# Attention scores as 64x64 products on quarters of the array, in place of 128x128 products on block-diagonal queries

## The chip, the cores and the metric

The kernel runs on one core of a Trainium2 chip. The metric is device time in microseconds, from the first to the last instruction of one execution as the chip reports it. Three runs of the kernel before took 924.23, 922.78 and 923.79 us, so the median is 923.79 us. Engine names are those of the profile: PE multiplies matrices (PEld is its weight load), DVE does elementwise work and reductions, ACT evaluates functions and copies, POOL is the general-purpose engine, and SP issues most transfers.

## The reference

Inputs are q, k and v of shape 8 x 8 x 576 x 64 (batch, heads, sequence, head dimension) in float32, and four weights in float64. The first step is windowed causal attention:

```
scores = scale * np.matmul(q, k.transpose(0, 1, 3, 2))
rel = pos[:, None] - pos[None, :]
mask = (rel >= 0) & (rel < 64)
scores = np.where(mask, scores, -1000000000.0)
scores = scores - np.max(scores, axis=-1, keepdims=True)
attn = np.exp(scores)
attn = attn / (np.sum(attn, axis=-1, keepdims=True) + 1e-09)
x = np.matmul(attn, v)
```

Its output, 8 batches of 576 tokens with 512 channels, goes through a token-mixing and then a channel-mixing network:

```
h = np.maximum(xt @ w_tok1, 0.0) @ w_tok2      # over the 576 tokens, hidden 256
u = x + h.transpose(0, 2, 1)
h2 = np.maximum(u @ w_ch1, 0.0) @ w_ch2        # over the 512 channels, hidden 1536
out = u + h2
```

## The kernel before

The work has two phases. The **first phase** does attention and token mixing, and converts the float64 weights to float32 pieces. The **second phase** is channel mixing, 9 chunks of 512 tokens, with products split into high and low parts (names ending in hi and lo).

In the first phase the sequence of each batch is cut into 9 blocks of 64 tokens. A **tile** holds two blocks on 128 partitions, rows 0-63 and rows 64-127 (`tile_blocks`), with all 8 heads; two batches make 9 tiles, and there are 36 tiles. Since the window is 64, a block of queries needs its own block of keys and the one before it, 128 keys.

- **Scores** (`qk`, L248-260). One product contracts over 128 partitions: partitions 0-63 hold the head dimension of the first block and partitions 64-127 that of the second. So that the two blocks do not mix, the queries are copied into `qbd`, a buffer that is block-diagonal: for each head 128 columns, the first 64 with the first block's queries on partitions 0-63, the last 64 with the second block's on partitions 64-127, and zeros elsewhere. The zeros are written once (L117, L118); the two copies per tile (`expand_q`, L155 and L156) are DVE's. A tile has 8 products, one for each head, in two halves u of 4 heads; each half fills one PSUM bank (tag "s", two buffers).
- **Softmax** (L262-287). For the first 7 tiles the mask is added on PE by a product (L255), later by DVE (L275); DVE takes the row maximum (L278, or L272 and L273), and ACT the exponentials (L286) with their sums.
- **Transposes** on PE (L293) with a copy by ACT (L295) give `pt`, and the product with v (`av`, L305) gives the tile's output `xp`. It is done as 16 products of 64 output rows, one for each head and block. DVE divides by the sums (L313, L314, L319).
- **Token mixing**: `split_x` splits the result (ACT L90, POOL L93), `tok1` (L349) and the *pieces* of `tok2` (L384, L391, copied out by ACT in L396) do the two products. A batch has 8 pieces, 4 of 256 tokens and 4 of 320; a tile does up to two, one behind its first transposes and one behind `av`.
- **Weights**: each tile converts one slice of the weights, on DVE in two parts (L187-189 and L198-201), then on POOL (L203) and on ACT and POOL (L90, L93).

Order is by hand: each engine executes what the loop over tiles (L448-531) records, in that order. An iteration i does the scores and softmax of tile i + 1 and the rest of tile i. On PE the order is: scores u = 0, transposes u = 0, a piece, scores u = 1, transposes u = 1, `tok1`, `av`, a piece. On ACT it is: copy of the first `pt`, casts, exponentials u = 0 of the next tile, copy of the piece, copy of the second `pt`, exponentials u = 1, copy of the second piece, cast of the tile's result. On DVE it is: mask and maximum u = 0, the two copies into `qbd`, reciprocal, first part of a weight slice, mask and maximum u = 1, second part of the slice, division. In the first four tiles both transposes come together and the copies into `qbd` come last.

Of the kernel before, what the change touches and what calls it, by code (L numbers as in the profile page):

```python
# [10 lines left out]
F32 = mybir.dt.float32  # L11
# [11 lines left out]
P = 128  # L23
BLK = 64
# [12 lines left out]
# Columns of a tile's keys that the first load brings, parts that the last product comes in.  # L37
K0 = P + BLK
# [20 lines left out]
# A batch's blocks in the order in which the kernel holds its tokens: tile t has blocks t and t + 4,  # L59
# the last block shares a tile with the other batch of its pair.  # L60
# [13 lines left out]
def mixer_kernel(ctx: ExitStack, tc: tile.TileContext, qh, kh, kr, vh, wt1, wt2, wc1, wc2, out):  # L74
# [34 lines left out]
    with ExitStack() as actx:  # L109
# [5 lines left out]
        qbd = [pq.tile([P, H, 2, BLK], F32, name=f"qbd{n}") for n in range(3)]  # L115
        def zero_q(qt, eng):
            eng.memset(qt[0:BLK, :, 1], 0.0)  # L117
            eng.memset(qt[BLK:P, :, 0], 0.0)  # L118

        zero_q(qbd[0], nc.vector)  # L120
        kbs, loaded, cpool = {}, {}, [pq]

        def load_k(i):
            p, t = divmod(i, TPP)
            if t == 4:
                kt = pq.tile([P, H, P], F32, name=f"kr{p}", tag="kr", bufs=1)
                nc.sync.dma_start(kt, kr[p])
                kbs[i] = kt
            elif t in (0, 5):
                b = 2 * p + (t == 5)  # L130
                kt = pq.tile([P, H, 5 * BLK], F32, name=f"k{b}", tag="k", bufs=2)
                if b != 0:
                    nc.sync.dma_start(kt, kh[b])
                for n in range(4):
                    kbs[i + n] = kt[:, :, n * BLK:n * BLK + P]
                return kt

        def load_q(i):
            qr = pq.tile([P, H, BLK], F32, name=f"q{i}", tag="q", bufs=3)
            if i == 0:  # L140
                for hs in (slice(0, 4), slice(4, H)):
                    nc.sync.dma_start(qr[:, hs], qh[i, :, hs])
                    nc.sync.dma_start(k0[:, hs, :K0], kh[0, :, hs, :K0])
            else:
                nc.sync.dma_start(qr, qh[i])
            loaded[i] = [qr, None]
# [5 lines left out]

        def expand_q(i, h0=0, h1=H):
            qr, qt = loaded[i][0], qbd[i % 3]
            nc.vector.tensor_copy(qt[0:BLK, h0:h1, 0], qr[0:BLK, h0:h1])  # L155
            nc.vector.tensor_copy(qt[BLK:P, h0:h1, 1], qr[BLK:P, h0:h1])  # L156
# [17 lines left out]
        zero_q(qbd[1], nc.gpsimd)  # L174
        zero_q(qbd[2], nc.gpsimd)
# [5 lines left out]
        def to_f32_a(raw, n, tag):  # L181
            """float64 words, low and high, to the nearest float32: its range, and the mantissa in place."""
# [10 lines left out]
        def to_f32_b(c, low, high, n, tag):  # L193
            """Its sign and exponent, and what the low word adds."""
# [11 lines left out]
        # Weights: (source, where its high and low parts or its float32 go, columns).  # L206
# [41 lines left out]
        def qk(i, u):  # L248
            qt, kt = qbd[i % 3], kbs[i]
            tag, bufs = ("up", 1) if i < N_PE and (2 * i + u) % 3 == 2 else ("s", 2)  # L250
            s = ps.tile([P, 4, P], F32, name=f"s{i}_{u}", tag=tag, bufs=bufs)
            on_pe = i < N_PE
            if on_pe:
                mk = maskr[1 if tile_blocks(i)[0][1] == 0 else 0]
                nc.tensor.matmul(s, identr, mk.unsqueeze(1).to_broadcast([P, 4, P]), start=True, stop=False,  # L255
                                 skip_group_check=True)
            for h in range(4):
                nc.tensor.matmul(s[:, h], qt[:, 4 * u + h].rearrange("p a q -> p (a q)"), kt[:, 4 * u + h],  # L258
                                 start=not on_pe, stop=True, skip_group_check=on_pe)
            s_ps[i, u] = s  # L260

        def softmax(i, u):  # L262
# [7 lines left out]
            nmu = nm[:, 4 * u:4 * u + 4]  # L270
# [9 lines left out]
        def softmax_exp(i, u):  # L280
# [3 lines left out]
            for h in range(4):  # L284
                g = 4 * u + h
# [14 lines left out]
        def av(i, pts):  # L300
            vt = loaded.pop(i)[1]
            xp = ps.tile([P, H, D], F32, name=f"xp{i}", tag="av", bufs=1)
            for h in range(H):
                for half in range(2):
                    nc.tensor.matmul(xp[half * BLK:(half + 1) * BLK, h],  # L305
                                     pts[h // 4][:, h % 4, half * BLK:(half + 1) * BLK],
# [141 lines left out]
        for i in range(-1, NT + 1):  # L448
# [14 lines left out]
            if i + 1 < NT:  # L463
                qk(i + 1, 0)
# [187 lines left out]
```

## Time and profile before

The profile is of one execution; its span is 923.1 us, and the median of the runs shown is 0.7 us above it.

| | us |
|---|---|
| median of 3 runs | 923.79 |
| lowest, highest | 922.78, 924.23 |
| span of the profiled execution | 923.1 |
| first `av` of the 36 | at 14.2 |
| last `av` of the 36 | at 295.8 |
| first product of the second phase | at 312.6 |
| PE, DVE, ACT, POOL busy in the span | 892.4, 425.6, 304.3, 134.0 |

A line of the timeline gives the start, the duration, the engine, the line of the program, the operation, what is written and read, the shapes, and how many instructions were merged (xN). A bracket at the end tells how long the engine sat idle before it and what released it. The line of a helper stands for all its uses, so L90 and L93 are the high and low parts of every split. The end of a PE instruction is modelled and overlaps the next; rates on PE are therefore taken from starts.

### The profile page before, as it was taken

What the parts mean: (1) busy time and instruction counts of PE and PEld (TensorE: products, weight loads), DVE (VectorE), ACT (ScalarE), POOL (GpSimd) and SP (SyncE); (2) the same over time, 40 slices, a digit from 0 to 9 for tenths busy, and PEclk for the clock granted to TensorE, in tenths of its full rate; (3) what the DMA queues carried; (4) which work ended last, traced back from release to release, by engine and by line L of the source; (5) the groups of instructions that cost most, each with busy time, mean ns of one, the idle gap of its engine ahead of it and who ended that gap; (6) DMA issues with size and microseconds to landing.
All of it is one profiled execution on the core that took longest, in us unless ns stands there. A gap on an engine that the chain in (4) does not pass through costs nothing.

```text
span 923.1 us, 13509 instructions
## 1 busy us (share of the span) xinstructions
PE 892.4 (97%) x5426; PEld 737.4 (80%) x5426; DVE 425.6 (46%) x762; ACT 304.3 (33%) x953; POOL 134.0 (15%) x134
## 2 busy tenths in 40 slices
PE   6899899899999988999999999999999999999998
PEld 5778788788888867888888888888888888888887
DVE  7999999999998494022131130130130120220210
ACT  5677677676776422021020020120120120120210
POOL 4334334433233162000000000000000000000000
PEclk9999999999999999999999999999999999999999
DMA  9556565765862640110200200100200100100000
GB/s 338 176 195 239 185 212 201 240 217 179 281 212 90 206 144 18 40 40 12 80 1 23 69 1 23 68 1 23 69 1 34 58 1 35 57 10 26 12 12 34
DMA packets 41661, 89.07 MB, mean 96 GB/s; under 512 B 5504, under 2 KB 19200, under 8 KB 39680
## 3 DMA queue, kind: packets, MB, share of 16 engines
q1 hardware_dynamic: 39488, 86.39, 27.8%
q10 hardware_dynamic: 2112, 1.84, 0.6%
q8 instruction: 42, 0.69, 0.3%
q14 instruction: 19, 0.16, 0.1%
HBM read 67.37 MB, written 20.84 MB: 96 GB/s over the span
## 4 chain that ended last, share of the span: by engine, by line
PE 71%; DVE 26%; issue 1%; ACT 1%; DMA 1%; POOL 0%; SPq 0%; DVEq 0%; ACTq 0%; POOLq 0%
PE op L609 32%; PE gp L575 30%; DVE nm L278 3%; DVE e L275 3%; PE up L391 3%; DVE qbd L156 3%; DVE qbd L155 2%; DVE c L198 2%; PE h L349 2%; DVE c L189 2%; DVE r L201 2%; DVE x L319 1%; DVE c L188 1%; PE s L258 1%; PE up L384 1%; DVE r L200 1%
## 5 line engine op out<-in xcount | busy, mean ns | idle before, releaser
L579 ACT ACTIVATE ghi<-gp 128x512 fp32r<-128x512 f32 x108 | 64.4, 598 | 464.1 <-PE gp L575 463.2
L575 PE MATMUL gp<-uhi,w1hi 128*128 128x512 f32 x432 | 171.0, 396 | 6.0 <-DVE glo L580 6.0
L575 PE MATMUL gp<-uhi,w1lo 128*128 128x512 f32 x432 | 173.6, 402 | 0.0
L575 PE MATMUL gp<-ulo,w1hi 128*128 128x512 f32 x432 | 171.4, 397 | 0.0
L609 PE MATMUL op<-glo,w2hi 128*128 128x512 f32 (+1 forms) x444 | 170.3, 384 | 0.0
L609 PE MATMUL op<-ghi,w2hi 128*128 128x512 f32 (+1 forms) x444 | 170.3, 384 | 0.0
L609 PE MATMUL op<-ghi,w2lo 128*128 128x512 f32 (+1 forms) x444 | 170.2, 383 | 0.0
L580 DVE SCALAR_TENSOR_TENSOR glo<-gp,ghi 128x512 fp32r<-128x512 f32 x108 | 74.4, 690 | 198.9 <-ACT ghi L579 198.8
L611 DVE TENSOR_TENSOR uf<-op,uf 128x512 f32<-128x512 f32 (+1 forms) x37 | 25.0, 677 | 263.6 <-PE op L609 263.6
L286 ACT ACTIVATE e<-e,nm 128x128 f32<-128x128 f32 x232 | 90.4, 391 | 54.9 <-DVE nm L278 54.9
L575 PEld LDWEIGHTS gp<-uhi,w1hi 128*128 128x128 f32 x432 | 81.8, 189 | 27.4 <-DVE glo L580 8.1
L575 PEld LDWEIGHTS gp<-ulo,w1hi 128*128 128x128 f32 x432 | 81.7, 189 | 20.9
L575 PEld LDWEIGHTS gp<-uhi,w1lo 128*128 128x128 f32 x432 | 81.7, 189 | 19.0
L609 PEld LDWEIGHTS op<-ghi,w2hi 128*128 128x128 f32 x444 | 83.4, 188 | 16.6
L609 PEld LDWEIGHTS op<-glo,w2hi 128*128 128x128 f32 x444 | 83.4, 188 | 16.5
L609 PEld LDWEIGHTS op<-ghi,w2lo 128*128 128x128 f32 x444 | 83.4, 188 | 16.5
L258 PE MATMUL s<-k,qbd 128*128 128x128 f32 x512 | 71.5, 284 | 4.4 <-DVE qbd L156 2.5
L258 PEld LDWEIGHTS s<-k,qbd 128*128 128x128 f32 x512 | 66.3, 199 | 7.4 <-DVE qbd L156 2.8
L203 POOL TENSOR_TENSOR w<-r,c 128x384 f32<-128x384 f32 (+1 forms) x39 | 38.7, 991 | 167.0 <-DVE r L201 142.8
L305 PEld LDWEIGHTS xp<-v,pt 128*64 128x64 f32 x1152 | 37.4, 140 | 13.3 <-issue 3.9
L93 POOL TENSOR_TENSOR xlo<-x,xhi 128x512 fp32r<-128x512 f32 x32 | 41.4, 1293 | 25.4 <-ACT xhi L90 25.1
L391 PE MATMUL up<-t2hi,hhi 128*128 128x320 f32 (+1 forms) x128 | 43.7, 342 | 0.0
(78 smaller groups left out, 1099.3 us busy)
## 6 DMA issues: line engine op xcount, KB each, us to landing
v<-vh SPq DMA_DIRECT2D x36, 512.0 KB, 3.7
raw<-wc SPq DMA_DIRECT2D x32, 384.0 KB, 4.2
q<-qh SPq DMA_DIRECT2D x35, 256.0 KB, 4.1
k<-kh SPq DMA_DIRECT2D x7, 1280.0 KB, 9.8
out<-uf SPq DMA_DIRECT2D x35, 256.0 KB, 2.4
uf<-u_dram SPq DMA_DIRECT2D x8, 1024.0 KB, 5.7
u_dram<-u SPq DMA_DIRECT2D x7, 512.0 KB, 3.5
kr<-kr SPq DMA_DIRECT2D x4, 512.0 KB, 5.4
```

Source lines behind the costliest of these rows:

```text
L93: eng_lo.tensor_sub(lo, src, hi.bitcast(F32))
L156: nc.vector.tensor_copy(qt[BLK:P, h0:h1, 1], qr[BLK:P, h0:h1])
L203: nc.gpsimd.tensor_add(w, rf, cf)
L258: nc.tensor.matmul(s[:, h], qt[:, 4 * u + h].rearrange("p a q -> p (a q)"), kt[:, 4 * u + h], start=not on_pe, stop=True, skip_group_check ...
L275: nc.vector.scalar_tensor_tensor(out=e, in0=s_ps.pop((i, u)), scalar=scale, in1=mk.unsqueeze(1).to_broadcast([P, 4, P]), op0=ALU.mult, op1 ...
L286: nc.scalar.activation(e[:, h], src[:, h], AF.Exp, bias=nm[:, g:g + 1], scale=by, accum_out=sm[:, g:g + 1])
L305: nc.tensor.matmul(xp[half * BLK:(half + 1) * BLK, h], pts[h // 4][:, h % 4, half * BLK:(half + 1) * BLK], vt[:, half, h], start=True, sto ...
L391: nc.tensor.matmul(up[:, :n], hx[:, cs], w[:, tt * S + s0:tt * S + s0 + n], start=False, stop=(k == 6), skip_group_check=True)
L575: nc.tensor.matmul(gp, w[:, ct * F + ft * P:ct * F + (ft + 1) * P], x[:, ct], start=(k == 0), stop=(k == 3 * NCT - 1))
L579: nc.scalar.activation(ghi, gp, AF.Relu)
L580: nc.vector.scalar_tensor_tensor(out=glo, in0=gp, scalar=0.0, in1=ghi.bitcast(F32), op0=ALU.max, op1=ALU.subtract)
L609: nc.tensor.matmul(op, w[:, ft, cs], x[:, cols], start=(k == 0), stop=(k == 3 * NFT - 1))
```

## The change

The host lays queries and keys out by the parity of the head: partitions 0-63 hold the even heads, partitions 64-127 the odd ones, each with all the blocks of a batch for the keys and both blocks of a tile for the queries. A score product now contracts over 64 partitions and has 64 query rows: it takes one quarter of the array, by the head's parity (which partitions are read) and by the block in the tile (which PSUM partitions are written). A tile has 16 such products of 64x64 with 128 keys moving, where it had 8 of 128x128. Both PSUM banks of a tile are filled in one go (even heads in one, odd heads in the other), ahead of the first transposes. `qbd`, its zeros, `expand_q` and the separate key tensor `kr` are gone; u now means parity, and `av` takes its heads alternately from the two `pt`.

```
-        def qk(i, u):
-            qt, kt = qbd[i % 3], kbs[i]
-            tag, bufs = ("up", 1) if i < N_PE and (2 * i + u) % 3 == 2 else ("s", 2)
-            s = ps.tile([P, 4, P], F32, name=f"s{i}_{u}", tag=tag, bufs=bufs)
...
-            for h in range(4):
-                nc.tensor.matmul(s[:, h], qt[:, 4 * u + h].rearrange("p a q -> p (a q)"), kt[:, 4 * u + h],
-                                 start=not on_pe, stop=True, skip_group_check=on_pe)
+        def qk(i):
+            qt, on_pe = loaded[i][0], i < N_PE
+            s = []
+            for u in range(2):
+                tag, bufs = ("up", 1) if on_pe and (2 * i + u) % 3 == 2 else ("s", 2)
+                s.append(ps.tile([P, 4, P], F32, name=f"s{i}_{u}", tag=tag, bufs=bufs))
+                s_ps[i, u] = s[u]
+                if on_pe:
+                    mk = maskr[1 if tile_blocks(i)[0][1] == 0 else 0]
+                    nc.tensor.matmul(s[u], identr, mk.unsqueeze(1).to_broadcast([P, 4, P]), start=True, stop=False,
+                                     skip_group_check=True)
+            for j in range(4):
+                for u in range(2):
+                    r = slice(u * BLK, (u + 1) * BLK)
+                    for half, (b, n) in enumerate(tile_blocks(i)):
+                        nc.tensor.matmul(s[u][half * BLK:(half + 1) * BLK, j], qt[r, j, half],
+                                         kbs[b][r, j, n * BLK:n * BLK + P],
+                                         start=not on_pe, stop=True, skip_group_check=on_pe)
...
-        def expand_q(i, h0=0, h1=H):
-            qr, qt = loaded[i][0], qbd[i % 3]
-            nc.vector.tensor_copy(qt[0:BLK, h0:h1, 0], qr[0:BLK, h0:h1])
-            nc.vector.tensor_copy(qt[BLK:P, h0:h1, 1], qr[BLK:P, h0:h1])
...
-                                     pts[h // 4][:, h % 4, half * BLK:(half + 1) * BLK],
+                                     pts[h % 2][:, h // 2, half * BLK:(half + 1) * BLK],
...
             if i + 1 < NT:
-                qk(i + 1, 0)
-            if i == -1:
-                expand_q(0, 4, H)
+                qk(i + 1)
...
-            if 0 <= i and i + 2 < NT and not early:
-                expand_q(i + 2)
...
-            if i + 1 < NT:
-                qk(i + 1, 1)
             if 0 <= i < NT and not early:
                 pts.append(pt_transpose(i, 1))
```

The loads follow: the keys of a batch come as one transfer of 1.3 MB (before, the same and one of 0.5 MB for each pair of batches), the query buffers are five in place of three, and the first tile's queries come in one transfer in place of two.

On PE, in one iteration in the middle of the first phase, the order before is this (s is a PSUM bank of scores, pp one of transposes, up that of a piece):

```order
L258 MATMUL s_0_2377<-k_1677,qbd_86 128x128 x4
L293 MATMUL pp_0_2382<-ident,e_0_2276 128x128 x4
L384 MATMUL up_0_2_2405<-ident,x_1766 128x128
L384 MATMUL up_0_2_2405<-ident,x_1884 128x128
L391 MATMUL up_0_2_2405<-t2hi,hhi_0_2200 128x256
L391 MATMUL up_0_2_2405<-t2lo,hhi_0_2200 128x256
L391 MATMUL up_0_2_2405<-t2hi,hlo_0_2201 128x256
L391 MATMUL up_0_2_2405<-t2hi,hhi_1_2204 128x256
L391 MATMUL up_0_2_2405<-t2lo,hhi_1_2204 128x256
L391 MATMUL up_0_2_2405<-t2hi,hlo_1_2205 128x256
L258 MATMUL s_1_2419<-k_1677,qbd_86 128x128 x4
L293 MATMUL pp_1_2424<-ident,e_1_2317 128x128 x4
```

and in the same iteration with the change, whose scores begin with these rows (two products on one row: the two blocks of one head) and end with these:

```order
L239 MATMUL s_0_2485<-k_1751,q_2230 64x128 x2
L239 MATMUL s_1_2486<-k_1751,q_2230 64x128 x2
...
L274 MATMUL pp_0_2503<-ident,e_0_2391 128x128 x4
L365 MATMUL up_0_2_2524<-ident,x_1846 128x128
L365 MATMUL up_0_2_2524<-ident,x_1970 128x128
...
L372 MATMUL up_0_2_2524<-t2hi,hlo_1_2309 128x256
L274 MATMUL pp_1_2538<-ident,e_1_2425 128x128 x4
```

The first two rows alternate four times. The scores of the second half have moved ahead of the first transposes and of the piece, and nothing stands any more between the piece and the second transposes.

On DVE the rows from one tile's division to the first part of the weight slice are, before,

```order
L319 TENSOR_TENSOR x_2467<-xp_2450,ri_2396 128x512
L275 SCALAR_TENSOR_TENSOR e_0_2504<-s_0_2490,mask_84 128x512
L278 TENSOR_REDUCE nm_2502<-e_0_2504 128x4
L155 COPY qbd_88<-q_2375 64x8x64
L156 COPY qbd_88<-q_2375 64x8x64
L313 TENSOR_SCALAR ri_2509<-sum_2390 128x8
L314 RECIPROCAL ri_2509<-ri_2509 128x8
L187 TENSOR_SCALAR c_2530<-raw_2371 128x384
```

and with the change

```order
L300 TENSOR_TENSOR x_2463<-xp_2446,ri_2394 128x512
L256 SCALAR_TENSOR_TENSOR e_0_2512<-s_0_2485,mask_84 128x512
L259 TENSOR_REDUCE nm_2510<-e_0_2512 128x4
L294 TENSOR_SCALAR ri_2515<-sum_2390 128x8
L295 RECIPROCAL ri_2515<-ri_2515 128x8
L162 TENSOR_SCALAR c_2534<-raw_2356 128x384
```

Here the two copies are gone and all else stands as it stood. The order on ACT is the same in both kernels, and POOL loses only four of its first instructions.

More of the change, by code (lines that the diff above doesn't have):

```diff
@@ L36 @@
 CW = 384
-K0 = P + BLK
 LAST_PARTS = 2
@@ L73, in mixer_kernel @@
 @with_exitstack
-def mixer_kernel(ctx: ExitStack, tc: tile.TileContext, qh, kh, kr, vh, wt1, wt2, wc1, wc2, out):
+def mixer_kernel(ctx: ExitStack, tc: tile.TileContext, qh, kh, vh, wt1, wt2, wc1, wc2, out):
     nc = tc.nc
@@ L114, in mixer_kernel @@
         mask = [pa.tile([P, P], F32, name=f"mask{m}") for m in range(2)]
[L115 to L120, printed above, removed]
         kbs, loaded, cpool = {}, {}, [pq]
@@ L124, in load_k @@
             p, t = divmod(i, TPP)
[L125 to L131, printed above, removed]
+            if t in (0, 4):
+                b = 2 * p + (t == 4)
+                kbs[b] = pq.tile([P, H // 2, (NBLK + 1) * BLK], F32, name=f"k{b}", tag="k", bufs=2)
                 if b != 0:
[L133 to L136, printed above, removed]
+                    nc.sync.dma_start(kbs[b], kh[b])
         def load_q(i):
[L139 to L145, printed above, removed]
+            qr = pq.tile([P, H // 2, 2, BLK], F32, name=f"q{i}", tag="q", bufs=5)
+            nc.sync.dma_start(qr, qh[i])
             loaded[i] = [qr, None]
@@ L172, in mixer_kernel @@
             nc.scalar.activation(maskr[m], mask[m], AF.Copy, scale=NEG_PE / NEG)
-        zero_q(qbd[1], nc.gpsimd)
-        zero_q(qbd[2], nc.gpsimd)
         t1hi = pa.tile([P, 5 * DT], F32R, name="t1hi")
@@ L246, in mixer_kernel @@
         s_ps, e_sb, st = {}, {}, {}
-        def qk(i, u):
-            qt, kt = qbd[i % 3], kbs[i]
-            tag, bufs = ("up", 1) if i < N_PE and (2 * i + u) % 3 == 2 else ("s", 2)
-            s = ps.tile([P, 4, P], F32, name=f"s{i}_{u}", tag=tag, bufs=bufs)
[L252 to L256, printed above, removed]
-            for h in range(4):
-                nc.tensor.matmul(s[:, h], qt[:, 4 * u + h].rearrange("p a q -> p (a q)"), kt[:, 4 * u + h],
-                                 start=not on_pe, stop=True, skip_group_check=on_pe)
-            s_ps[i, u] = s
+        def qk(i):
[16 more added lines that the diff above has]
+                                         start=not on_pe, stop=True, skip_group_check=on_pe)
         def softmax(i, u):
@@ L269, in softmax @@
             e_sb[i, u] = e
-            nmu = nm[:, 4 * u:4 * u + 4]
+            nmu = nm.rearrange("p (j u) -> p j u", u=2)[:, :, u]
             if i < N_PE:
@@ L284, in softmax_exp @@
             for h in range(4):
-                g = 4 * u + h
+                g = 2 * h + u
                 nc.scalar.activation(e[:, h], src[:, h], AF.Exp, bias=nm[:, g:g + 1], scale=by,
@@ L431, in run_pieces @@
                 tok2(*pieces.pop(0))
-        k0 = load_k(0)
+        load_k(0)
         load_q(0)
+        k0, kh0 = (x[:, :, :8 * BLK].rearrange("p j (g n) -> p j g n", g=2) for x in (kbs[0], kh[0]))
+        for g in range(2):
+            nc.sync.dma_start(k0[:, :, g, :P], kh0[:, :, g, :P])
         job_load()
@@ L437, in mixer_kernel @@
         load_v(0)
-        nc.sync.dma_start(k0[:, :, K0:], kh[0, :, :, K0:])
+        for g in range(2):
+            nc.sync.dma_start(k0[:, :, g, P:], kh0[:, :, g, P:])
+        nc.sync.dma_start(kbs[0][:, :, 8 * BLK:], kh[0, :, :, 8 * BLK:])
         load_q(2)
@@ L441, in mixer_kernel @@
         load_v(1)
-        expand_q(0, 0, 4)
         tok1_plan, n = {}, 0
@@ L472, in mixer_kernel @@
                 softmax(i + 1, 0)
-            if 0 <= i and i + 2 < NT and not early:
-                expand_q(i + 2)
-            if early:
-                if i < 0:
-                    expand_q(i + 2)
-                if i > 0:
-                    norm(*normed.pop())
+            if early and i > 0:
+                norm(*normed.pop())
             if 0 <= i < NT:
@@ L501, in mixer_kernel @@
             if early:
-                if i >= 0:
-                    expand_q(i + 2)
                 for _ in range(n_jobs):
@@ L625 @@
     ji = np.array([[x[1] for x in tile_blocks(i)] for i in range(NT)])
-    qh = qb[bi, ji].transpose(0, 1, 4, 3, 2).reshape(NT, P, H, BLK)
-    kh = np.stack([kb[:, 0:5], kb[:, 4:9]], 1).transpose(0, 1, 5, 4, 2, 3).reshape(B, P, H, 5 * BLK)
-    kr = kb[:, 8:10].transpose(0, 4, 3, 1, 2).reshape(NPAIR, P, H, P)
+    qh = qb[bi, ji].reshape(NT, 2, BLK, H // 2, 2, D).transpose(0, 4, 5, 3, 1, 2).reshape(NT, P, H // 2, 2, BLK)
+    kh = kb.reshape(B, NBLK + 1, BLK, H // 2, 2, D).transpose(0, 4, 5, 3, 1, 2).reshape(B, P, H // 2, (NBLK + 1) * BLK)
     vw = np.stack([vb[bi, ji], vb[bi, ji + 1]], 2).reshape(NT, 2, P, H, D)
@@ L636 @@
     wc2 = wc2.reshape(NFT, P, C).transpose(1, 0, 2).reshape(P, NFT * C)
-    host = {"qh": qh, "kh": kh, "kr": kr, "vh": vh, "wt1": wt1, "wt2": wt2, "wc1": wc1, "wc2": wc2}
+    host = {"qh": qh, "kh": kh, "vh": vh, "wt1": wt1, "wt2": wt2, "wc1": wc1, "wc2": wc2}
     nc = bacc.Bacc("TRN2", target_bir_lowering=False, num_devices=1, dynamic_dma_scratch_size=1024)
```

## The prediction

> **What bounds the kernel now.** First the slices of the span, 23 us each (PE, DVE and ACT).
>
> ```profile
> PE   6899899899999988999999999999999999999998
> DVE  7999999999998494022131130130130120220210
> ACT  5677677676776422021020020120120120120210
> ```
>
> DVE is full for 13 slices, 300 us; PE is full from there on. The change touches only the first phase, so the 610 us behind it (its first product starts in the third row below) stay. The chain that ended last says the same by line:
>
> ```profile
> PE 71%; DVE 26%; issue 1%; ACT 1%; DMA 1%; POOL 0%; SPq 0%; DVEq 0%; ACTq 0%; POOLq 0%
> 150.00:200.00 50.00, 47.15 (x472) 40.71 (x471) 47.85 (x92) 34.45 (x130) 19.29 (x18) 1.00 0.64 208
> 312.56 0.40 PE L575 MATMUL gp<-uhi,w1hi 128*128 128x512 f32 x1
> ```
>
> The second row is a stretch of the first phase: PE 47.15, weight loads 40.71, DVE 47.85, ACT 34.45, POOL 19.29 of 50 us, clock 1.00, transfers 0.64. So DVE ends last, but ACT has 69% and PE is not idle: a gain on DVE soon meets another engine. The pace is read from the first `av` instruction of tiles 0, 6, 33 and 35 (some windows cut the count):
>
> ```profile
> 14.20 1.15 PE L305 MATMUL xp<-v,pt 128*64 128x64 f32 x32
> 61.31 0.28 PE L305 MATMUL xp<-v,pt 128*64 128x64 f32 x2
> 282.20 0.39 PE L305 MATMUL xp<-v,pt 128*64 128x64 f32 x6
> 295.78 0.39 PE L305 MATMUL xp<-v,pt 128*64 128x64 f32 x6
> ```
>
> Tiles 0-5 take (61.31 - 14.20) / 6 = 7.85 us each; tiles 6-32 take 220.9 / 27 = 8.18; the last two 6.8. One tile on DVE, with POOL beside it:
>
> ```profile
> 173.31 0.68 DVE L319 TENSOR_TENSOR x<-xp,ri 128x512 f32<-128x512 f32 x1
> 173.91 0.68 DVE L275 SCALAR_TENSOR_TENSOR e<-s,mask 128x512 f32<-128x512 f32 x1
> 174.63 0.69 DVE L278 TENSOR_REDUCE nm<-e 128x4 f32<-128x512 f32 x1
> 174.73 1.28 POOL L93 TENSOR_TENSOR xlo<-x,xhi 128x512 fp32r<-128x512 f32 x1 [0.25 <-ACT xhi L90]
> 175.23 1.05 DVE L155 COPY qbd<-q 64x512 f32<-64x512 f32 x1
> 175.96 1.20 POOL L93 TENSOR_TENSOR w1lo<-w,w1hi 128x384 fp32r<-128x384 f32 x1
> 176.29 1.15 DVE L156 COPY qbd<-q 64x512 f32<-64x512 f32 x1
> 177.48 0.17 DVE L313 TENSOR_SCALAR ri<-sum 128x8 f32<-128x8 f32 x1
> 177.80 0.31 DVE L187 TENSOR_SCALAR c<-raw 128x384 int32<-128x384 int32 x1
> 178.15 0.36 DVE L188 TENSOR_SCALAR c<-c 128x384 f32<-128x384 f32 x1
> 181.66 0.68 DVE L319 TENSOR_TENSOR x<-xp,ri 128x512 f32<-128x512 f32 x1
> ```
>
> The period is 181.66 - 173.31 = 8.35 us, with no idle time of DVE in it. The copies take 175.23 to 177.48, 2.25 us.
>
> **What is removed on DVE.** Two copies per tile go, but 2.25 us is not what they cost by themselves. Where POOL is idle they look like this:
>
> ```profile
> 15.92 0.41 DVE L155 COPY qbd<-q 64x512 f32<-64x512 f32 x1
> 16.34 0.42 DVE L156 COPY qbd<-q 64x512 f32<-64x512 f32 x1
> ```
>
> That is 0.83 us. In the tile above each copy ends 0.27 us after the POOL instruction under way ends (176.01, 177.16): 1.4 us of the 2.25 is a wait for POOL. The wait can pass on to what now stands there, the reciprocal's addition (L313) and the first weight operation. If it does, DVE gets past L187 0.22 us behind POOL's second instruction, at 177.38, instead of 178.15 (the start of L188); the period is 8.35 - 0.77 = **7.58 us**. If the wait vanishes it is 8.35 - 2.25 = 6.10. I take 7.58 for tiles with a weight slice: the POOL instructions depend on the division ahead of these rows and not on the copies, so they come where they came.
>
> The Trainium skill ("SBUF — State Buffer", section "SBUF: two separate sides") calls this port pair an exclusive lock held for a whole instruction. By that rule the wait passes on, and the trace agrees: both copies end just behind POOL's instructions.
>
> **What is changed on PE.** The scores of half a tile, and when DVE may read them:
>
> ```profile
> 261.65 1.05 PE L258 MATMUL s<-k,qbd 128*128 128x128 f32 x8
> 262.74 0.69 DVE L275 SCALAR_TENSOR_TENSOR e<-s,mask 128x512 f32<-128x512 f32 x1 [0.32 <-PE s L258]
> 179.79 1.05 PE L258 MATMUL s<-kr,qbd 128*128 128x128 f32 x8
> 180.68 0.60 PE L293 MATMUL pp<-ident,e 128*128 128x128 f32 x4
> ```
>
> Eight instructions, two for each of 4 products, take 180.68 - 179.79 = 0.89 us, 0.111 each; a tile 1.78. DVE starts 1.09 us after the first. With the change 8 heads and 2 blocks give 16 products of 64x64, hence 32 instructions in place of 16, each with the same 128 moving columns, so 0.111 us for its quarter. How many quarters work at once is not in the trace; the bounds are: one at a time 32 x 0.111 = 3.55 us, two 1.78, four 0.89. The nearest rows are those of `av`, which uses halves of the array for the two blocks:
>
> ```profile
> 177.72 0.28 PE L305 MATMUL xp<-v,pt 128*64 128x64 f32 x2
> 177.72 1.15 PE L305 MATMUL xp<-v,pt 128*64 128x64 f32 x32
> 178.80 0.44 PE L384 MATMUL up<-ident,x 128*128 128x128 f32 x2
> ```
>
> With 64 moving columns an instruction alone would take half of 0.111; 32 would take 1.78 us. They take 178.80 - 177.72 = 1.08, so two run at once, 0.93 us if two take 0.058, and 0.15 is left for changing the shape of the array. The first row, a window of 30 ns, shows two begun in it. The program gives both instructions of a product to the same half, one behind the other; two begun within 30 ns must be on different halves, so the second half did not wait for the first to finish its pair. On this I take **four at once**, 0.89 us, plus 0.15 for each of two changes of shape: 1.19 us in place of 1.78.
>
> The Trainium skill speaks against it: "TensorE: Matmul & The Clock Gate", section "Part 3: Packing small matmuls — row/col tiling", says that products start and end strictly in program order. By that rule only neighbours on different quarters overlap, two at a time, and the time is that of the first rival; the 30 ns row does not agree with it, and no run here shows quarters.
>
> **Which loop then ends last.** PE, DVE and ACT stand in a ring. Rows not shown so far:
>
> ```profile
> 175.44 0.40 ACT L286 ACTIVATE e<-e,nm 128x128 f32<-128x128 f32 x1
> 177.00 0.35 ACT L396 COPY u<-up 128x256 f32<-128x256 f32 x1
> 177.25 0.58 ACT L295 COPY pt<-pp 128x512 f32<-128x512 f32 x1
> 182.28 0.64 PE L384 MATMUL up<-ident,x 128*128 128x128 f32 x3 [1.00 <-ACT u L396]
> 183.83 1.05 PE L258 MATMUL s<-kr,qbd 128*128 128x128 f32 x8
> ```
>
> ACT copies the second `pt` of tile i only after the exponentials of tile i + 1, since its order is fixed; `av` needs that copy, now from its first product on (heads alternate). So: scores until DVE reads 1.09 (all four rounds end together); mask and maximum until the first exponential 175.44 - 173.91 = 1.53; four exponentials 177.00 - 175.44 = 1.56; copy of the piece 0.25; copy of `pt` 0.58; 0.1 to hand over (as between the maximum's end, 175.32, and 175.44); `av` 1.08; the next piece 179.79 - 178.80 = 0.99 with 256 tokens, or 183.83 - 182.28 = 1.55 with 320; change of shape 0.15. Sums: 7.33 us and 7.89 us. Before, this ring had 0.15 less and hid under DVE's 8.35.
>
> Of 9 tiles, 4 have two pieces of 256 (DVE's 7.58 ends last), 4 two of 320 (7.89), and one has none or no slice (I take 7.0, between DVE's 6.10 and 7.58): (4 x 7.58 + 4 x 7.89 + 7.0) / 9 = **7.65 us** against 8.18. The gain is 27 x 0.53 = 14.3 us. Tiles 0-5 have no pieces; DVE loses at least 0.83 and PE's change of shape gives 0.15 back, 6 x 0.68 = 4.1 (bounds 0 and 6 x 2.25 - 0.9 = 12.6; nearer the low one, as ACT's exponentials and copies follow at once). The last two tiles: 1.0. The start gains nothing, since it waits for transfers of the same size. Sum: 923.1 - 14.3 - 4.1 - 1.0 = 903.7; the median of runs lies 0.7 above the span: **904.4**.
>
> The edits that cost nothing: zeros (POOL, DVE) run before the first scores while transfers are under way; fewer key bytes, on queues that are 0.64 busy; more query buffers. The doubled instructions of `qk` are priced above. Were a key transfer late (a batch's keys are now needed one tile earlier, four tiles after their issue, some 30 us), it would hold PE, and with it DVE's e; nothing in the rows is near that.
>
> **Rivals.**
>
> *Two quarters at a time.* The pair of instructions of a product blocks the quarter behind it, and the scores take 1.78 + 0.30 us. DVE reads 0.89 later, since both banks fill together, and the ring becomes 8.22 and 8.78; mean (4 x 8.22 + 4 x 8.78 + 7.6) / 9 = 8.40, 0.22 over today's: 27 x 0.22 = +5.9, first tiles 6 x (0.89 - 0.68) = +1.3, last +0.5: **931.5, slower**. It decides from a block of 0.89 + 0.53 = 1.42 us on. For it: nothing in the trace shows quarters apart by their rows. Against it: the 30 ns row. One at a time would be the ring 2.66 longer, 27 x (10.1 - 8.18) + 6 x 2.0 = +64, about 988.
>
> *PE alone bounds.* If ACT's order does not hold PE up and POOL's wait vanishes, PE's own work remains: scores 1.19, two transposes 0.9, `tok1` 1.40 (row below), `av` 1.23, two pieces 1.98 or 3.10: 6.7 and 7.8, with a tile without pieces 4.7, mean 6.98. Gain 27 x 1.20 + 4.1 + 1.0 = 37.5: **886**. Against it: the ring is made of orders that stay.
>
> ```profile
> 257.69 1.40 PE h L349 x6
> ```
>
> *No change.* Ring and DVE add up instead of overlapping, and each tile loses 0.5 us: within 0.2% of 923.8, which is about what a measurement of this kernel can tell from no change.
>
> **How the numbers follow.** Chances: forecast 0.60 (own range 895 to 914: rings 0.3 either way over 33 tiles), PE alone 0.10, no change 0.05, two quarters 0.22, one at a time 0.03. So faster 0.70, same 0.05, slower 0.25. The range is 889 to 935: it leaves out most of the PE-alone case, the upper part of the two-quarter case and one at a time, under 0.2 together.
>
> **What would show it.** Scores of a tile: 32 instructions begun in about 0.9 us, DVE's e about 1.1 to 1.2 us behind the first; 1.8 us would be the first rival. `av` starting right behind the second `pt` copy with PE idle ahead of it shows the ring; L313 and L187 longer than 0.17 and 0.31 us show the wait for POOL passed on. `av` to `av` should be 7.6 to 7.9 us. A DVE still full, or PE full through the first phase, would make the forecast wrong.

## The result

The kernel after takes 902.35 us (median of 4 runs, 901.16 to 902.97) against 924.01 us (median of 4 runs on the same chip, 922.78 to 924.50). The ratio is 0.9766, with a 95% interval of 0.9753 to 0.978. The prediction was 904.4 us. The profiled execution has a span of 899.2 us, and its own time is 901.16 us.

The page of the kernel after, with the slices of the span (22.5 us each) and the chain of work that ended last:

```profile
PE   7889999999999989999999999999999999999998
DVE  5989979988883870130220220230220220220210
ACT  5777778787774240120120120120120220210210
...
PE 80%; DVE 14%; ACT 4%; issue 1%; DMA 0%; POOL 0%; SPq 0%; DVEq 0%; ACTq 0%
```

DVE is no longer full in the first phase, PE nearly is, and DVE's part of the chain went from 26% to 14%. The same stretch of the first phase as before (busy us of PE, weight loads, DVE, ACT, POOL, then clock, transfers):

```profile
150.00:200.00 50.00, 48.16 (x614) 38.44 (x614) 44.61 (x85) 39.62 (x149) 22.30 (x20) 1.00 0.71 226
```

The timeline of PE, at the first `av` instruction of tiles 0, 6 and 33, and at the first product of the second phase:

```profile
15.61 0.38 PE L286 MATMUL xp<-v,pt 128*64 128x64 f32 x2
57.92 0.28 PE L286 MATMUL xp<-v,pt 128*64 128x64 f32 x2
260.32 0.28 PE L286 MATMUL xp<-v,pt 128*64 128x64 f32 x2
290.00 0.40 PE L549 MATMUL gp<-uhi,w1hi 128*128 128x512 f32 x1
```

With the same points of the kernel before, the 923.1 - 899.2 = 23.9 us between the two spans divide like this:

| stretch | before | after | difference | predicted |
|---|---|---|---|---|
| start, to the first `av` | 14.2 | 15.6 | +1.4 | 0 |
| tiles 0-5 | 47.1 | 42.3 | -4.8 | -4.1 |
| tiles 6-32 | 220.9 | 202.4 | -18.5 | -14.3 |
| from tile 33 to the second phase | 30.4 | 29.7 | -0.7 | -1.0 |
| second phase | 610.5 | 609.2 | -1.3 | 0 |

The second phase is untouched by the change. Its 1.3 us go with the clock: in two stretches of 10 us (335 to 345 and 345 to 355 us) the kernel before was granted 0.83 of it on average, the kernel after in one (315 to 325 us).

### The profile page after: what moved, and what is told of

It is laid out like the page before. It is cut to its first block, busy times and chain, and to the rows that moved or that the text cites. A ratio compares the mean times of both kernels' runs of the same rounds, so it can differ in the third digit from the quotient of the medians.

```text
span 899.2 us, 14591 instructions
## 1 busy us (share of the span) xinstructions
PE 871.6 (97%) x6002; PEld 704.7 (78%) x6002; DVE 381.5 (42%) x686; ACT 305.0 (34%) x953; POOL 129.5 (14%) x130
## 4 chain that ended last, share of the span: by engine, by line
PE 80%; DVE 14%; ACT 4%; issue 1%; DMA 0%; POOL 0%; SPq 0%; DVEq 0%; ACTq 0%
PE op L583 33%; PE gp L549 31%; PE up L372 4%; PE s L239 3%; PE xp L286 3%; PE h L330 3%; ACT e L267 2%; DVE nm L259 2%; DVE e L256 2%; PE up L365 2%; DVE c L173 2%; PE pp L274 1%; DVE c L162 1%; DVE c L164 1%; ACT pt L276 1%
## 5 line engine op out<-in xcount | busy, mean ns | idle before, releaser
L286 PEld LDWEIGHTS xp<-v,pt 128*64 128x64 f32 x1152 | 39.4, 139 | 21.0 <-ACT pt L276 8.7
L286 PE MATMUL xp<-v,pt 128*64 128x64 f32 x1152 | 47.0, 229 | 5.8 <-ACT pt L276 5.0
L276 ACT COPY pt<-pp 128x512 f32<-128x512 f32 x72 | 41.7, 583 | 13.1 <-PE pp L274 12.8
L239 PE MATMUL s<-k,q 64*64 64x128 f32 x1152 | 43.3, 284 | 2.1 <-DVE c L173 1.6
L256 DVE SCALAR_TENSOR_TENSOR e<-s,mask 128x512 f32<-128x512 f32 x58 | 39.6, 683 | 13.2 <-PE s L239 13.1
```

The lines of the kernel that those rows point to most:

```text
L239: nc.tensor.matmul(s[u][half * BLK:(half + 1) * BLK, j], qt[r, j, half], kbs[b][r, j, n * BLK:n * BLK + P], start=not on_pe, stop=True, sk ...
L256: nc.vector.scalar_tensor_tensor(out=e, in0=s_ps.pop((i, u)), scalar=scale, in1=mk.unsqueeze(1).to_broadcast([P, 4, P]), op0=ALU.mult, op1 ...
L276: nc.scalar.copy(pt, pp)
L286: nc.tensor.matmul(xp[half * BLK:(half + 1) * BLK, h], pts[h % 2][:, h // 2, half * BLK:(half + 1) * BLK], vt[:, half, h], start=True, sto ...
```

## One tile after the change

DVE, with POOL beside it, in the timeline of the kernel after:

```profile
156.36 0.68 DVE L256 SCALAR_TENSOR_TENSOR e<-s,mask 128x512 f32<-128x512 f32 x1
159.81 0.69 DVE L256 SCALAR_TENSOR_TENSOR e<-s,mask 128x512 f32<-128x512 f32 x1
160.53 0.69 DVE L259 TENSOR_REDUCE nm<-e 128x4 f32<-128x512 f32 x1
160.63 1.29 POOL L92 TENSOR_TENSOR xlo<-x,xhi 128x512 fp32r<-128x512 f32 x1 [0.24 <-ACT xhi L89]
161.13 0.81 DVE L294 TENSOR_SCALAR ri<-sum 128x8 f32<-128x8 f32 x1
161.87 1.01 POOL L92 TENSOR_TENSOR w1lo<-w,w1hi 128x384 fp32r<-128x384 f32 x1
162.10 1.00 DVE L162 TENSOR_SCALAR c<-raw 128x384 int32<-128x384 int32 x1
163.14 0.36 DVE L163 TENSOR_SCALAR c<-c 128x384 f32<-128x384 f32 x1
163.81 0.68 DVE L256 SCALAR_TENSOR_TENSOR e<-s,mask 128x512 f32<-128x512 f32 x1
```

In this tile the wait for POOL passed on to the two instructions that the prediction named: L294 takes 0.81 us (0.17 before), L162 takes 1.00 (0.31 before). Together that is 1.33 us of wait, where the copies had 1.4. DVE begins L163 at 163.14, which is 0.26 us behind the end of POOL's second instruction; the prediction had 0.22. From the second mask of one tile (156.36) to that of the next (163.81) it is 7.45 us, and the timeline marks no idle time of DVE between them.

The scores of that tile on PE, in windows that end 30, 200 and 320 ns behind the first, and then whole:

```profile
158.38 0.34 PE L239 MATMUL s<-k,q 64*64 64x128 f32 x4
158.38 0.45 PE L239 MATMUL s<-k,q 64*64 64x128 f32 x8
158.38 0.56 PE L239 MATMUL s<-k,q 64*64 64x128 f32 x12
158.38 1.10 PE L239 MATMUL s<-k,q 64*64 64x128 f32 x32
```

Four instructions begin at once, and four more with each further step: the starts in the trace are 0, 7, 13 and 20 ns, then 160 to 180, 269 to 289, 378 to 398, and so on by 109 ns. From the first start to the last it is 0.835 us in every tile after the first two but one (in tile 7 the block stops behind its first four). The two instructions of one product are neighbours in program order on the same quarter, so the second waits for the first, and the three other quarters start all the same.

The ring through PE and ACT in the same tile, from `av` to the next `av`:

```profile
155.70 0.58 ACT L276 COPY pt<-pp 128x512 f32<-128x512 f32 x1
155.88 1.49 PE L286 MATMUL xp<-v,pt 128*64 128x64 f32 x32
157.30 0.44 PE L365 MATMUL up<-ident,x 128*128 128x128 f32 x2
161.35 0.40 ACT L267 ACTIVATE e<-e,nm 128x128 f32<-128x128 f32 x1
162.90 0.36 ACT L377 COPY u<-up 128x256 f32<-128x256 f32 x1
163.15 0.58 ACT L276 COPY pt<-pp 128x512 f32<-128x512 f32 x1
163.32 0.34 PE L286 MATMUL xp<-v,pt 128*64 128x64 f32 x4
```

As predicted, `av` comes with the second copy of `pt` (163.15), which comes behind the exponentials and the copy of the piece. It does not wait for the copy's end, though: its first four instructions use the first `pt` alone.

## Experiments

Five questions are open: which part of the change brought the gain, how four quarters work at once, what ends last in the tile now, what the start lost, and whether DVE was the bound of the kernel before. Each ratio is to runs of the kernel before on the same chip, whose medians lie between 923.2 and 923.4 us (924.01 in the result above).

**The copies alone, put back.** The kernel after, with the two copies per tile where they stood, into a buffer that nobody reads.

```diff
+        def copy_q(i):
+            qr, qt = loaded[i][0].rearrange("p j a q -> p (j a) q"), spare[i % 2]
+            nc.vector.tensor_copy(qt[0:BLK, :, 0], qr[0:BLK])
+            nc.vector.tensor_copy(qt[BLK:P, :, 1], qr[BLK:P])
...
                 softmax(i + 1, 0)
+            if 0 <= i and i + 2 < NT and not early:
+                copy_q(i + 2)
```

> The changed kernel with the two DVE copies per tile put back, into a buffer that no product reads; the scores stay on quarters. Theory (the copies were what ended last): the copies take up the wait for POOL again that L294 and L162 took over, so a tile on DVE goes from 7.45 us back to about 8.2, and the 27 middle tiles cost 27 x 0.68 = 18 us, the first six about 5: 922 to 926 us. Rival (the gain came from the shorter scores on PE): the copies fit beside PE's work, at most 906 us.

Measured: 928.46 us, ratio 1.0053 (1.0036 to 1.0071). Many middle tiles take 8.34 to 8.38 us, and tiles 6-32 take 8.22 on the mean, against 8.18 before the change. The copies have their old length beside POOL, and the reciprocal behind them is short again; DVE in the timeline of this kernel:

```profile
160.47 1.07 DVE L120 COPY spare<-q 64x512 f32<-64x512 f32 x1
161.55 1.15 DVE L121 COPY spare<-q 64x512 f32<-64x512 f32 x1
162.73 0.17 DVE L300 TENSOR_SCALAR ri<-sum 128x8 f32<-128x8 f32 x1
```

So without the removal of the copies nothing is gained, although the scores are on quarters. It is 2.5 us above the upper end of what was expected, which goes with the clock: its seven runs were granted 0.987 to 0.992 on the mean, the kernel before 0.994 to 0.998, and its fastest run, at 0.992, took 925.5 us.

**The copies alone, taken away.** The kernel before with no copies from tile 3 on, so 128x128 products on the queries of earlier tiles.

```diff
             qr, qt = loaded[i][0], qbd[i % 3]
+            if i > 2:
+                return
             nc.vector.tensor_copy(qt[0:BLK, h0:h1, 0], qr[0:BLK, h0:h1])
```

> The kernel before without its copies from the fourth tile on: later tiles multiply the queries of the first three, so the output is wrong, and everything else is as before, with 128x128 products in two halves. Theory: DVE falls to 7.45 us as in the changed kernel; tiles with two pieces of 320 tokens meet PE, 8.27 us from av to av in the profile before (259.02 to 267.29); mean (4 x 7.45 + 4 x 8.25 + 7.2) / 9 = 7.78 us, 27 x 0.28 = 7.6 us over the changed kernel, less 1.4 us at the start: about 908 us, so the quarters are worth about 6 us and the copies about 15. Rival 1 (the quarters add nothing): 901 to 903 us. Rival 2 (the quarters are half of the gain or more): 912 us or more.

Measured: 905.97 us, ratio 0.9808 (0.9794 to 0.9823). The copies are worth 17.4 us in this order of the work (923.41 on the same chip), the quarters some 4 us on top. In tiles 6-32 the quarters bring more, 7.70 - 7.50 = 0.20 us a tile or some 5.5 in all; the start takes part of it back, for the first `av` comes at 13.2 us here and at 15.6 in the kernel after.

**The order of the products.** All eight instructions of a quarter in a row (16 products in the order u, half, head), in place of two in a row:

```diff
-            for j in range(4):
-                for u in range(2):
-                    r = slice(u * BLK, (u + 1) * BLK)
-                    for half, (b, n) in enumerate(tile_blocks(i)):
+            for u in range(2):
+                r = slice(u * BLK, (u + 1) * BLK)
+                for half, (b, n) in enumerate(tile_blocks(i)):
+                    for j in range(4):
```

> The changed kernel with the same 16 score products in another order: the four heads of one quarter in a row, then the next quarter. In the profile of the changed kernel four instructions begin within 20 ns on the four quarters, and the next four 109 ns later. Theory A (each quarter has a queue of its own, filled far enough ahead): the order does not matter, the 32 instructions still begin within 0.84 us, 902 us. Theory B (PE looks only a few instructions ahead): four products of one quarter run one after the other and hold back the next quarter, up to 32 x 0.111 = 3.55 us for a tile, 2.6 us more on the ring and some 70 us on the kernel: up to 972 us; in between if it looks some way ahead.

Measured: 950.85 us, ratio 1.0287 (1.0241 to 1.0332). The block now takes 2.295 us from the first start to the last, which is between the two theories. The timeline in windows that end 0.48 and 0.55 us behind the first start, and the whole:

```profile
155.10 0.65 PE L239 MATMUL s<-k,q 64*64 64x128 f32 x4
155.10 0.81 PE L239 MATMUL s<-k,q 64*64 64x128 f32 x6
155.10 2.56 PE L239 MATMUL s<-k,q 64*64 64x128 f32 x32
```

In the first 0.48 us only the first quarter's first four run (starts at 0, 160, 269 and 378 ns). The second quarter's first begins at 493 ns, 6 ns behind the fifth of the first quarter (487). This fits a PE that looks ahead over one running and about three waiting instructions of a quarter, where a fourth waiting one stops everything behind it.

Four in a row, two products instead of one, test that limit:

```diff
-            for j in range(4):
-                for u in range(2):
-                    r = slice(u * BLK, (u + 1) * BLK)
-                    for half, (b, n) in enumerate(tile_blocks(i)):
+            for j2 in range(2):
+                for u, half, j in [(u, half, 2 * j2 + k) for u in range(2) for half in range(2) for k in range(2)]:
+                        b, n = tile_blocks(i)[half]
+                        r = slice(u * BLK, (u + 1) * BLK)
```

> The kernel after, with two products (four instructions) in a row for each quarter instead of one product (two instructions). If a quarter can hold some three waiting instructions beside the one that runs, as the order quarter by quarter showed with eight in a row, four in a row still start together: 32 instructions begun in 0.8 to 0.9 us, 901 to 904 us. Rival, the limit is lower (one or two waiting): each quarter's block holds up the next by one to two instructions of 0.109 us, the 32 take 1.1 to 1.6 us, and the time is 907 to 920 us.

Measured: 906.38 us, ratio 0.9817 (0.98 to 0.9833). The block takes 0.898 us instead of 0.835. The first four of all quarters begin in step (0, 14, 27 and 40 ns and so on to 488, 501, 514 and 528); only at the fifths the quarters fall apart, 597 for the first and 654, 667, 680 for the others. So four in a row fit, with 57 ns to pay where a quarter's next group follows. When the fourth quarter's first one begins at 40 ns, nine instructions of the other quarters are waiting, so the limit of three counts for each quarter. Of the 4 us, at most 36 x 0.063 = 2.3 are this (tiles 6-32 are 0.05 us longer, 1.3 in all); the rest goes with a lower granted clock (0.989 to 0.992 in its runs, 0.994 to 0.997 in those of the kernel after), whose cause stays open.

**A longer score block.** Each score product issued twice from tile 7 on:

```diff
+                        if not on_pe:
+                            nc.tensor.matmul(s[u][half * BLK:(half + 1) * BLK, j], qt[r, j, half],
+                                             kbs[b][r, j, n * BLK:n * BLK + P], start=True, stop=True)
```

> The changed kernel with each score product issued twice from the eighth tile on, the second overwriting the first with the same values: a block of scores of twice the length, 1.75 us in place of 0.88, as two quarters at a time would give. Theory (the ring of scores, maximum, exponentials, second copy of pt, av and piece ends last): the 0.88 us come on top in every middle tile, 27 x 0.85 = 23 us: 922 to 926 us, about the time of the kernel before. Rival (PE's own work bounds, the ring has slack): 256-token tiles 7.6 and 320-token tiles 8.65, mean 7.85, 27 x 0.35 = 9 us: about 911 us.

Measured: 929.39 us, ratio 1.0063 (1.0048 to 1.0078). That is 3.4 us above the expected range, but on the side of the ring. From its first start to its last the block is now 1.86 us long, 1.02 more than 0.835, and the tiles are 1.0 us longer (8.75 and 8.81 where the kernel after has 7.73 and 7.78). DVE's masks now wait for the scores 46.1 us in all, against 13.1 before the doubling; the groups of the two kernels, first after, then this one, with the idle time ahead of the instruction as last column:

```profile
L256 DVE SCALAR_TENSOR_TENSOR e<-s,mask 128x512 f32<-128x512 f32 x58 | 39.6, 683 | 13.2 <-PE s L239 13.1
```

```profile
L259 DVE SCALAR_TENSOR_TENSOR e<-s,mask 128x512 f32<-128x512 f32 x58 | 39.8, 685 | 46.1 <-PE s L243 46.1
```

So time in the scores is on the path that ends last, nearly one for one. It also prices the first rival: with the quarters two at a time the block would be about as long as here (1.78 us), and the rival's 931.5 us were about right for its case.

**Two changes of order.** On DVE, mask and maximum of both halves ahead of the reciprocal and the weight slice:

```diff
                 softmax(i + 1, 0)
+                if not early:
+                    softmax(i + 1, 1)
...
-            if i + 1 < NT:
+            if i + 1 < NT and early:
                 softmax(i + 1, 1)
```

> The changed kernel with DVE's order altered after the first four tiles: mask and maximum of both parities come one behind the other, and the reciprocal and the first part of the weight slice behind them. Both banks of scores are ready at once now, and the mask and maximum rows show no wait for POOL (0.68 and 0.69 us with POOL under way), so POOL's two instructions run beside them. DVE's tile loses the wait, 0.65 us in L294 and 0.70 in L162: 7.45 to about 6.1. Theory (the ring through ACT and PE ends last close behind DVE, 7.33 and 7.75 us): 12 tiles gain about 0.12 us and the others nothing, 900 to 902 us. Rival (DVE alone held the middle tiles): they gain up to what PE needs, 27 x 0.4 = 11 us: about 891 us.

Measured: 902.52 us, ratio 0.9771 (0.9746 to 0.9796). On PE, both transposes ahead of the first piece, so that the second `pt` is ready earlier:

```diff
                 pts.append(pt_transpose(i, 0))
-                if early:
-                    pts.append(pt_transpose(i, 1))
+                pts.append(pt_transpose(i, 1))
...
-            if 0 <= i < NT and not early:
-                pts.append(pt_transpose(i, 1))
```

> The changed kernel with both transposes of a tile one behind the other in every tile, as in the first four: ACT copies the second pt ahead of the next tile's exponentials, so av no longer waits for them and the ring is open. DVE's order stays, 7.45 us a tile with the wait for POOL. Theory (ring and DVE are of nearly the same length): tiles of 256 tokens stay at 7.45, tiles of 320 tokens stay at PE's 7.75, 900 to 903 us. Rival (the ring alone ends last): PE's own 6.98 on average, 27 x 0.5 = 14 us: about 889 us.

Measured: 902.76 us, ratio 0.9769 (0.9749 to 0.9789). By these medians neither alone gains on the 902.35 us of the kernel after; in the profiles tiles 6-32 take 7.47 and 7.42 us on the mean against 7.50, which is 0.8 and 2.0 us in all. Both together, the same two edits in one kernel:

> The changed kernel with both alterations of order: maxima of both parities first on DVE, both transposes first on PE and ACT. Theory (each of the two hides behind the other): now PE's own work is left, 6.9 us in tiles of 256 and 7.75 in tiles of 320 tokens, mean about 7.2; 27 x 0.3 = 8 us, more than the two apart give together: 892 to 896 us. Rival (something else is as long, ACT with 40 of 50 us busy): no more than the better of the two apart.

Measured: **891.01 us**, ratio 0.9651 (0.9634 to 0.9668), better than the kernel after by 11.3 us and a little better than expected (tiles 6-32 take 7.16 us). DVE of the first of the two kernels with one edit, then of the second:

```profile
162.94 0.69 DVE L256 SCALAR_TENSOR_TENSOR e<-s,mask 128x512 f32<-128x512 f32 x1 [0.55 <-PE s L239]
```

```profile
154.85 1.16 DVE L162 TENSOR_SCALAR c<-raw 128x384 int32<-128x384 int32 x1
162.44 1.15 DVE L162 TENSOR_SCALAR c<-raw 128x384 int32<-128x384 int32 x1
```

With the maxima first, DVE idles 0.55 us for the scores: the ring through PE and ACT sets the pace. With the transposes first, DVE has its wait for POOL and a period of 162.44 - 154.85 = 7.59 us: DVE and POOL set it. Each hides the gain of the other. With both, PE is left, busy for 49.56 of 50 us:

```profile
150.00:200.00 50.00, 49.56 (x653) 39.81 (x651) 43.20 (x91) 41.56 (x160) 21.81 (x20) 1.00 0.68 224
```

**The same two orders in the kernel before.** The copies stay, right behind the maxima; both score blocks move ahead of both transposes.

```diff
                 qk(i + 1, 0)
+                if not early:
+                    qk(i + 1, 1)
...
                 pts.append(pt_transpose(i, 0))
-                if early:
-                    pts.append(pt_transpose(i, 1))
+                pts.append(pt_transpose(i, 1))
...
                 softmax(i + 1, 0)
+                if not early:
+                    softmax(i + 1, 1)
```

> The kernel before, with both changes of order at once (both score blocks and both transposes ahead of the pieces on PE, both masks and maxima first on DVE); the copies of q stay. If DVE's own work ends last in the kernel before (8.35 us per tile with the copies and their wait for POOL), an order on PE, DVE and ACT can't shorten it: 919 to 926 us, DVE still full in the first phase. Rival, the orders are worth their 11 us whatever else stands in the kernel: 910 to 914 us.

Measured: 910.17 us, ratio 0.9854 (0.9838 to 0.987). My theory missed and the rival holds: the orders gain 13.2 us without the change. DVE and POOL in the timeline of this kernel:

```profile
158.24 0.68 DVE L319 TENSOR_TENSOR x<-xp,ri 128x512 f32<-128x512 f32 x1
158.84 0.68 DVE L275 SCALAR_TENSOR_TENSOR e<-s,mask 128x512 f32<-128x512 f32 x1
159.56 0.69 DVE L278 TENSOR_REDUCE nm<-e 128x4 f32<-128x512 f32 x1
159.66 1.29 POOL L93 TENSOR_TENSOR xlo<-x,xhi 128x512 fp32r<-128x512 f32 x1 [0.24 <-ACT xhi L90]
160.16 0.68 DVE L275 SCALAR_TENSOR_TENSOR e<-s,mask 128x512 f32<-128x512 f32 x1
160.88 0.69 DVE L278 TENSOR_REDUCE nm<-e 128x4 f32<-128x512 f32 x1
161.08 1.01 POOL L93 TENSOR_TENSOR w1lo<-w,w1hi 128x384 fp32r<-128x384 f32 x1
161.48 0.90 DVE L155 COPY qbd<-q 64x512 f32<-64x512 f32 x1
162.39 0.42 DVE L156 COPY qbd<-q 64x512 f32<-64x512 f32 x1
165.84 0.68 DVE L319 TENSOR_TENSOR x<-xp,ri 128x512 f32<-128x512 f32 x1
```

Mask (L275) and maximum (L278) run at their own length beside POOL's instructions. Moved to where POOL works, they cover it, and of the 1.4 us of wait 0.5 is left in this tile, in the first copy. Over tiles 6-32 the copies take 10.6 us more than the 0.83 a tile that they take alone, where in the kernel before they took 29.0 more. DVE's period falls from 8.35 to 165.84 - 158.24 = 7.60 us, with all its work still in it. PE is nearly full here too, 49.60 of 50 us:

```profile
150.00:200.00 50.00, 49.60 (x484) 42.33 (x483) 47.65 (x95) 40.31 (x148) 22.09 (x20) 1.00 0.71 243
```

The Trainium skill ("SBUF — State Buffer", section "SBUF: two separate sides") says which DVE instructions take the lock: those in a mode with two ports, or with two inputs from SBUF. By that, a mask that reads its scores from PSUM and a reduction need not wait, and these rows agree. The prediction had read only the other half of the rule.

So the change is worth about the same in both orders, but by different parts of it:

| | as it stands | with both orders | middle tile |
|---|---|---|---|
| before | 924.0 | 910.2 | 8.18, 7.75 |
| after | 902.4 | 891.0 | 7.50, 7.16 |
| difference | -21.7 | -19.2 | -0.68, -0.60 |

In the order as it stands it is mostly the copies; with both orders PE is nearly full on either side, and the shorter scores are what is left to count. The prediction's 1.78 - 1.19 = 0.59 us per tile is close to the 0.60 of the last column.

**The start.** In the first microseconds PE waits for a PSUM bank (the first row below). The second tile's scores are given banks of another tag:

```diff
                 tag, bufs = ("up", 1) if on_pe and (2 * i + u) % 3 == 2 else ("s", 2)
+                if 2 * i + u in (3, 4):
+                    tag, bufs = "h", 2
```

> The changed kernel with two PSUM banks that are free in the first tiles (tag h, first used by token mixing in the third iteration) for the odd scores of the second tile and the even ones of the third. In the changed kernel PE stands 1.85 us ahead of the second tile's scores for a bank that ACT's exponentials hold, and the first av comes at 15.6 us, 1.4 later than before. Theory: the first av comes at 14.2 us or earlier and the kernel gains 1 to 2 us, 900.5 to 901.5. Rival (transfers or the slow clock of the start set the first av): no gain.

Measured: 903.93 us, ratio 0.9785 (0.9767 to 0.9803); the first `av` comes at 15.6 us as before. PE and its weight loads in the timeline of the kernel after, then PE in this one:

```profile
10.38 0.79 PE L233 MATMUL s<-maskr,identr 128*128 128x512 f32 x1 [1.85 <-ACT e L267]
11.11 2.67 PE L239 MATMUL s<-k,q 64*64 64x128 f32 x32
11.80 1.57 PEld L239 LDWEIGHTS s<-k,q 64*64 64x64 f32 x30 [0.41 <-DMA k<-kh]
13.71 1.97 PE L274 MATMUL pp<-ident,e 128*128 128x128 f32 x8
18.55 1.10 PE L239 MATMUL s<-k,q 64*64 64x128 f32 x32
```

```profile
10.95 2.79 PE L241 MATMUL s<-k,q 64*64 64x128 f32 x32 [2.18 <-DMA k<-kh]
```

The rival of the expectation holds. With the bank free, the first of the same scores wait for their keys instead, until 10.95 us, and all but the first product wait for more keys in both kernels: 30 of the 32 weight loads begin at 11.80 us in the kernel after and at 11.76 here. Behind that, PE runs slowly in both: 1.97 us for 8 transposes that take 1.09 later, in steps of 0.213 us where later ones have 0.109, and the last 30 scores begin within 1.56 us of each other, where later all 32 begin within 0.835. The traces' first record of a full granted clock is at 11.4 us in the kernel before and at 17.5 in the kernel after; it is at 9.7 and 9.9 us in the two other kernels with the old start and between 15.0 and 20.4 in the others with the new one. Why it comes later with the new start is not shown.

## Why the prediction was right, point by point

- **DVE ends last, and the copies leave: right for this order.** The copies put back bring the old time, the copies taken away nearly the new one. In the tile shown DVE still ends last, 7.45 us where 7.58 were forecast. But DVE's 8.35 us held 1.4 us of wait that the order of the work decides; that "DVE ends last" was a property of the order, not of DVE's work, and I saw that only in the last experiment.
- **The wait for POOL passes on: right in the tile shown, half right over all.** There it is 1.33 us on L294 and L162. But over tiles 6-32 the copies took 29.0 us more than the 0.83 a tile that they take alone, and after the change L294 and L162 take 8.3 and 7.0 us more than their 0.17 and 0.31: L162 waits in ten of its 24 places only. DVE's busy time there fell by 34.7 us and the time by 18.5 only, so in many tiles DVE no longer ends last.
- **Four quarters at once, 0.89 us: right.** 0.835 us from first to last start. The change of shape costs 0.09 us on either side (0.200 us from the last score to the first transpose, where scores are 0.109 apart), not 0.15. The rule of strict program order in the Trainium skill ("TensorE: Matmul & The Clock Gate", section "Part 3: Packing small matmuls — row/col tiling"), which carried the first rival, does not hold here for starts: the third instruction, on another quarter, begins 153 ns ahead of the second, which waits behind the first on its own. The order quarter by quarter shows how far it goes: three waiting instructions of a quarter are passed, a fourth is not.
- **The ring: right in kind, its steps mis-sized.** The tile shown takes 163.32 - 155.88 = 7.44 us from `av` to `av`, where the ring had 7.33. Its steps: `av` 1.42 (1.08 expected), piece and change of shape 1.08 (1.14), scores until DVE reads 1.43 (1.09), mask to exponential 1.54 (1.53), exponentials 1.55 (1.56), the rest 0.42 (0.93). The last step was mis-sized: `av` starts its first four instructions on the first `pt` and loses 0.26 us to the second one inside, so its beginning overlaps the copy; `av` and the rest together are 0.17 shorter than forecast. And DVE reads 0.34 later, since it is still at the division: without this wait for DVE the ring would take some 7.1, and DVE, with no idle time, sets the 7.44.
- **The mean of the middle tiles, 7.65 us: mis-sized, 7.50 measured.** Two terms were off. DVE's 7.58 is 7.45 in the tile shown, because POOL's second instruction takes 1.01 us there (1.20 in the tile of the prediction), and in tiles where L162 does not wait DVE needs less still. And the tiles were sorted wrongly: of nine tiles from tile 16 on, two have two pieces of 256 tokens (7.45 and 6.54 us), two have two of 320 (7.78 and 8.06, where 7.89 were expected for four tiles), three have one of each (7.73, 7.71 and 7.44) and two have one piece alone (7.23 and 7.75). No run separates the two terms. Together they make 4.2 of the 4.5 us by which the span is shorter than forecast.
- **First tiles, 0.68 us each: 0.80 measured.** That is near the 0.83 of the copies by themselves, from which the lower price was made. The kernel without copies from tile 3 on takes 42.9 us for these tiles, against 47.1 before and 42.3 after, so most of it is the copies. The kernel before had a stretch of 3.4 us at half the clock in tile 5, which the kernel after had not; that tile's difference (8.87 against 8.65 us) may be due to it.
- **The start gains nothing: wrong by 1.4 us.** The step named the transfers, and they do hold the second tile's scores, all but the first product until 11.8 us. It left out that PE is slow behind them. The loss varies: the first `av` comes at 13.2 to 14.2 us in three profiles with the old start, at 15.5 to 16.0 in eight with the new one (18.0 in the order quarter by quarter).
- **The rivals.** One and two quarters at a time fall by the starts of the scores. "PE alone bounds", 886 us, did not come by the change itself; the kernel with both orders comes near that case, at 891.0. "No change" falls by the 21.7 us.

## What to carry to other kernels

An engine that the profile shows as full may be full of waits: look for instructions that are longer in one place than in another, see which engine they end with, and ask whether instructions that don't wait for it can stand there instead. Where two loops are within some per cent of each other, a change to one alone can show next to nothing, as here; try the two together before either is called worthless. Here products on quarters of the array needed an order in which no quarter gets more than four instructions (two float32 products) in a row.

## What was not expected of the hardware

Quarters do run past a waiting neighbour, but only over some three of its instructions: the same 32 instructions take 0.835, 0.898 or 2.295 us by their order alone.

The granted clock halves for several microseconds inside a busy first phase, in some runs and not in others. The row of the kernel with the maxima first:

```profile
50.00:60.00 10.00, 9.71 (x75) 6.92 (x76) 7.19 (x15) 7.43 (x30) 2.27 (x2) 0.51 0.44 149
```

Its tile 5 took 12.2 us where the kernel after has 8.65, and its runs range from 900.09 us at a mean clock of 0.996 to 904.42 at 0.991. What sets the clock back at that place stays open; a difference of less than some 3 us between two of these kernels can't be read without it.
